# A Fourier token mixer with a hardswish MLP on one core: when the inverse transform's last stage runs, and where its two copies stand on ScalarE

## The chip, the cores and the metric

One core of one Trainium2 chip runs the whole kernel in float32. The metric is the device time in microseconds (us) of one execution. Engines are named as the profile names them: PE is TensorE (PEld its weight loads), ACT is ScalarE, DVE is VectorE, POOL is GpSimd, SP is SyncE, whose queue issues most of the DMAs.

## The reference, cut to what matters

```
x: 8 x 3008 x 256, filt_r and filt_i: 1505 x 256
y = irfft(rfft(x, axis=1) * (filt_r + 1j * filt_i), n=3008, axis=1)
t = y.reshape(24064, 256)
h = t @ w_in                               # 256 x 2048
g = h * clip(h + 3, 0, 6) / 6
out = g @ w_out                            # 2048 x 256
```

## The kernel before, in words

**The MLP sets the pace.** The 24064 tokens go in 47 blocks of 512 (256 pairs of tokens), numbered 0 to 46, and the 2048 hidden columns in 8 slices of 256. One block with one slice is a *step*; the steps 0 to 7 of a block follow each other, 376 in all. Both products of a step are done as 2x2 block products with seven multiplications (Strassen's scheme); block 0 alone is done plainly. The main loop (L1100 to L1160) writes each engine's order out by hand: within a step, the first product's parts for this step (`up_1` to `up_5`) alternate with the second product's parts for the step before (`down`). In PE's order: `up_1` (three products, into the PSUM tiles al and be), the early items of the plan (see below), `down` 1, `up_2` (two products), `down` 2 and 4, `up_3` (one product), `down` 5 and 6, `up_5` (one product, the "A22 product"), `down` 7 and 3.

The other engines' part of a step:

- ACT: L699 and L700 copy al and a half of be after `up_1`, L709 copies al after `up_2`; `relu(0)` (L733) follows in `up_4`; L728 copies al after the A22 product and `relu(1)` (L733) follows.
- DVE: first what the step before still owes, `g_sums`: hswish of the second half (L738) and the sums of g (L745, L746, L748). Then L714 (be plus s gives h, which `relu(0)` reads), L719 (al plus s5), and hswish of the first half (L738). The A22 product overwrites al, so it waits until L719 has read it.

**The mixer runs inside the MLP's steps.** The transform of length 3008 = 47 x 64 is done in stages for one of the eight sequences while the MLP works on the one before. A plan (`at(step, ...)`, L896) hangs its units on steps: an *early* item is issued after `up_1`, the others at the step's end. The units are:

- first stage: `a_unit` (PE, ACT), `a_sums` (DVE), `z_store` (four DMA issues on POOL's queue);
- second stage: `b_unit` (PE into two PSUM banks of the pool psF), `f_unit` (the filter: L515, L516, L517 on DVE, which read the banks and one operand in SBUF), `y_unit` (L526, L527 on DVE, both operands in SBUF), `bi_unit` (PE into two psF banks, two ACT copies) and `g_store` (DMA issues on POOL);
- last stage: `t4_load` (SP), then `n_five` for a chunk of five columns (5 x 47 pairs) or `n_unit` for a smaller one.

`n_five` takes both banks of psF, does 80 small products (L628), copies the two banks into the ring xn with ACT (`ring`, L610: two copies, or four where the ring wraps), and where the chunk completes a block it calls `ready`, which runs `t_sums` on POOL: seven additions (L684, tile xt) that the block's MLP steps need. The first of them reads the halves that both copies write. All of it is early, so the two copies stand in ACT's order between L700 and L709.

psF has two banks in all; `b_unit`, `bi_unit`, `a_unit`, `n_unit` and `n_five` take turns on them.

**Where the chunks stand.** Each block has a letter (`kinds`): the six blocks ahead of a new sequence are c, a, A, B, A, B, others count as a. A and B are the blocks in which the second stage stands: in A, `b_unit` at steps 2 and 6, `f_unit` at 2, 3, 6, 7, `y_unit` at 4 and 5; in B, `b_unit` at 4, `f_unit` at 4 and 5, `y_unit` at 2, 3, 6, 7, and `bi_unit` at 0 and 6 (and at step 1 of the A block that follows). `FIVE_AT` (L1029) gives the step of a five-column chunk by the letter: a chunk alone in its block, the first of two, the second of two. There are 46 such chunks: 12 in A blocks at step 4, 9 in B blocks at step 2, one in a B block (block 37) at step 3, the others in blocks of other letters or first of two.

In block 1 POOL also forms the sums of the weights (`w_sums`: L361 on POOL, L364 on ACT, which waits for L361); they stand at the ends of steps.

Of the kernel before, what the change touches and what calls it, by code (L numbers as in the profile page):

```python
# [34 lines left out]
B = 8  # L35
# [16 lines left out]
PAIRS = BLK // 2  # L52
# [129 lines left out]
def kernel(  # L182
# [64 lines left out]
    st = {}  # L247
# [330 lines left out]
    def pair(i):  # L578
        b, js, o, n = chunks[i]
        return b * HC * NA + o, n  # L580
# [24 lines left out]
    def ring(i, a, m_, to, out, src):  # L605
        done = 0
        while done < m_:
            r = (chunks[i][0] * HC * NA + to + done) % RING
            m = min(m_ - done, RING - r)
            nc.scalar.activation(out=out(ds(r, m)), in_=src[:, :, ds(a + done, m)], func=AXT.Copy)  # L610
            done += m

    def ready(i):
        t, n = pair(i)
        if (t + n) // PAIRS > t // PAIRS > 0:
            t_sums(t // PAIRS)


    def n_five(i):
        b, js, o, n = chunks[i]  # L620
        s0 = i % 2 * NJ
        ps = [psF.tile([P, 512], FP32, name="psn", tag="f")[:, 0:2 * n].rearrange("p (e n) -> p e n", e=2) for c in range(2)]
        for q, j in enumerate(js):
            for dh in range(2):
                for g in range(2):
                    for c in range(2):
                        r = ds(c * HALF, ATOM)
                        nc.tensor.matmul(ps[c][ts(g, HALF), dh, ts(q, NA)], t4[r, s0 + q, ds(dh * P + g * HALF, HALF)],  # L628
                                         groups[r, j, :], start=True, stop=True)
        for c in range(2):  # L630
            ring(i, 0, n, o, lambda at_: xn[:, :, c, at_], ps[c])
        ready(i)

    def n_unit(i, dh):
        ps = psF.tile([P, 512], FP32, name="psn", tag="f")
# [41 lines left out]
    def t_sums(k):  # L677
        t = xtp.tile([P, 5, PAIRS], FP32, name="xt")
        c0, s0, c1, s1 = (xb(k, d, c) for d in range(2) for c in range(2))
        u, v = (t[:, i, :] for i in (F5, F3))  # L680
        f1, f2, f3, f4, f5 = (t[:, i, :] for i in (F1, F2, F3, F4, F5))
        for o, x0, x1, op_ in ((f1, c0, s0, ALU.subtract), (u, c0, c1, ALU.add), (v, s0, s1, ALU.add),
                               (f4, u, v, ALU.subtract), (f5, u, v, ALU.add), (f2, c1, s1, ALU.add), (f3, f1, f2, ALU.add)):
            nc.gpsimd.tensor_tensor(out=o, in0=x0, in1=x1, op=op_)  # L684
        st["xt", k] = t

    def product(ps, p, w, x, start=False, stop=False):
        nc.tensor.matmul(ps, w_in[p][:, w, :], x, start=start, stop=stop, skip_group_check=True)  # L688
# [14 lines left out]
    def up_2(k, p):  # L703
        t = st["xt", k]
        al, be, s, s5 = st["up"]
        h = [hp.tile([P, 512], FP32, name="h%d" % i) for i in range(2)]
        product(al, p, S2, t[:, F3, :])
        product(be[:, 1, :], p, S4, t[:, F5, :], stop=True)
        nc.scalar.activation(out=s[:, 1, :], in_=al, func=AXT.Copy)  # L709
        st["h"] = h  # L710
# [10 lines left out]
    def up_4(k, p):  # L721
        st["g", k, p] = gp.tile([P, 7, 256], FP32, name="g")
        relu(0)
# [7 lines left out]
    def relu(i):  # L731
        r = rp.tile([P, 512], FP32, name="r", tag="r")
        nc.scalar.activation(out=r, in_=st["h"][i], func=AXT.Relu, bias=half_c, scale=1.0 / 6.0)  # L733
        st["r", i] = r
# [33 lines left out]
    def last_down():  # L768
        p, v, add = NP - 1, nc.vector.tensor_tensor, ALU.add
        g, o = st["g", LAST, p], st["o", LAST][0]  # L770
        hswish(LAST, p, 1)
        ps = [psF.tile([P, 512], FP32, name="psf", tag="f") for t in range(2)]
        for i, a in ((0, G11), (1, G12)):
            for t in range(2):
                for u in range(2):
                    nc.tensor.matmul(ps[t][:, ts(u, D)], g[:, a + t, ts(u, P)],
                                     w_out[p][:, 2 * i:2 * i + 2, :].rearrange("p j m -> p (j m)"),
                                     start=i == 0 and u == 0, stop=i == 1, skip_group_check=True)
        out_4(LAST)
        v(out=o_at(LAST, 0, 1), in0=st["po", LAST][3][:, 1, :, :], in1=o_at(LAST, 0, 1), op=add)  # L780
        for t, qs in ((0, (nc.sync, nc.gpsimd, nc.scalar)), (1, (nc.sync, nc.scalar))):
            both = o[:, t, :, :].rearrange("p u d -> p (u d)")
            v(out=both, in0=ps[t], in1=both, op=add)
            store_last(t, qs)
# [6 lines left out]
    def plain_up(p):  # L791
        st["g", 0, p] = gp.tile([P, 7, 256], FP32, name="g")
        st["h"] = [psU.tile([P, 512], FP32, name=n) for n in ("al", "be")]
        for i in range(2):
            for d in range(2):
                nc.tensor.matmul(st["h"][i], w_in[p][:, 2 * d + i, :], xn[:, d, :, 0:PAIRS], start=d == 0, stop=d == 1)
            relu(i)
            hswish(0, p, i)

    def plain_down(p):  # L800
        g = st["g", 0, p]
        if p == 0:
            st["po", 0] = [psO.tile([P, 2, 2, P], FP32, name="po%d" % i) for i in range(2)]
        for t in range(2):
            for u in range(2):
                for i, a in ((0, G11), (1, G12)):
                    nc.tensor.matmul(st["po", 0][t][:, u, :, :].rearrange("p a m -> p (a m)"), g[:, a + t, ts(u, P)],
                                     w_out[p][:, 2 * i:2 * i + 2, :].rearrange("p j m -> p (j m)"),
                                     start=p == 0 and u == 0 and i == 0, stop=p == NP - 1, skip_group_check=True)
# [82 lines left out]


    EARLY = (a_unit, b_unit, bi_unit, n_unit, n_five)

    def at(step, fn, *a):  # L896
        plan.setdefault((step, fn in EARLY), []).append((fn, a))

    with tc.manual_schedule():
# [126 lines left out]
                kinds[first[n] - 7 + d] = kind  # L1026

        N_AT = {"c": ((6, 6), (3, 3), (6, 6)), "a": ((2, 4), (2, 4), (6, 6)), "A": ((4, 5), (1, 1), (4, 5)), "B": ((2, 3), (1, 1), (2, 3))}
        FIVE_AT = {"c": (6, 3, 6), "a": (4, 2, 4), "A": (4, 0, 4), "B": (2, 1, 3)}  # L1029
        N_FIRST = {0: ((3, 4),), 1: ((), (2, 2), (3, 3)), 2: ((1, 1),), 3: ((1, 1),)}  # L1030
        in_block = {}
        for i in range(2, len(chunks)):
# [2 lines left out]
        for i in range(2, len(chunks)):  # L1035
# [3 lines left out]
            at_, kind = same.index(i) + 1 if len(same) > 1 else 0, kinds.get(k - 1, "a")  # L1039
            steps = N_FIRST[k - 1][at_] if k - 1 in N_FIRST else (FIVE_AT[kind][at_],) * 2 if len(chunks[i][1]) == NJ else N_AT[kind][at_]  # L1040
            if head and len(same) == 1:
# [58 lines left out]
        for i in range(len(items) + 1):  # L1100
            up = i < len(items)
            k, p = items[min(i, len(items) - 1)]
            dn = i > 0
            kd, pd = items[i - 1]
            def do(early):
                for fn, a in plan.get((i, early), ()):
                    fn(*a)

            if k == 0:
                plain_up(p)  # L1110
                do(True)
                if dn:
                    plain_down(pd)
                do(False)
                continue
            if not up:
                last_down()
                break
            up_1(k, p)
            ends = k == LAST and p == NP - 1  # L1120
            do(True)
            last_plain = dn and kd == 0
            dn = dn and kd > 0
            if dn:
                g_sums(kd, pd)
                down(kd, pd, 1)
            if up:
                up_2(k, p)
            if dn and pd == 0 and kd > 1:
                out_4(kd - 1)  # L1130
            if up:
                up_2b(k, p)
            if dn:
                down(kd, pd, 2, 4)
                if pd == NP - 1:
                    out_1(kd)
            if up:
                up_3(k, p)
            if dn:
                down(kd, pd, 5, 6)  # L1140
            if up:
                up_4(k, p)
            if ends:
                out_1(k)
            if last_plain:
                plain_down(pd)
                plain_out()
            if dn and pd == 0 and kd > 1:
                out_5(kd - 1)
            if up:  # L1150
                hswish(k, p, 0)
            if up:
                up_5(k, p)
            if dn:
                if pd == NP - 1 or ends:
                    out_2(kd)
                down(kd, pd, 7, 3)
                if pd == NP - 1 or ends:
                    out_3(kd)
            do(False)  # L1160
# [30 lines left out]
```

## Time and profile before

| what | value |
|---|---|
| three runs | 2677.99, 2678.18, 2678.54 us (median 2678.18) |
| the profiled execution | 2678.58 us, of which span 2676.8 us (first to last instruction) |
| granted PE clock | 1.000 |
| L733 ACT, relu, x736 | 721 ns each |
| L738 DVE, hswish, x736 | 716 ns each on average |
| L745, L746, L748 DVE, sums of g, x367 each | 470, 696, 435 ns on average |
| L526, L527 DVE, `y_unit`, x84 each | 810, 812 ns on average |
| L684 POOL, `t_sums`, x184 and x138 | 805, 1008 ns on average |
| L610 ACT, 128 x 470, x62 | 561 ns each |

How to read it: the profile's groups give the mean of one instruction; the timeline gives each instruction's start and duration in us from the start of the span ("x2" merges two in a row; in brackets stands the idle time before it and what ended it). The chain that ended last is followed back from the last instruction: at each step to what released it. A step begins with the first product of `up_1`, a PE row "al<-xt ... x2" that comes just ahead of a row "be<-xn"; the distance from one such row to the next is the step's length. A matmul's end is modelled.

### The profile page before, as it was taken

To read this page: it belongs to the slowest core of one execution; us is meant where nothing else is said; L and a number is where in the kernel's file an instruction comes from. 1 tells how busy PE (TensorE), PEld (TensorE's weight loads), DVE (VectorE), ACT (ScalarE), POOL (GpSimd) and SP (SyncE) were. 2 spreads that over 40 slices of the span, in tenths; PEclk is the share of its full clock that TensorE was granted. 3 is DMA by queue.
4 is the path that set the end of the run, shared out by engine and by line. 5 is a ranking of instruction groups with operands and counts; after the bars stand their busy time and mean duration, and the time that the engine had idled before them with its cause. 6 is when DMAs were issued, how large, how long until landed. Compare 5 with 4: busy or idle time off the path is not lost.

```text
span 2676.8 us, 54235 instructions
## 1 busy us (share of the span) xinstructions
PE 2646.1 (99%) x21584; PEld 2317.4 (87%) x21584; DVE 2062.9 (77%) x3503; ACT 1303.9 (49%) x2672; POOL 509.7 (19%) x731
## 2 busy tenths in 40 slices
PE   8999999999999999999999999999999999999999
PEld 6588888888888888888888888888888888899998
DVE  7878877887678876788767887678887788866666
ACT  3344454444544454444554444545454454454554
POOL 2251122111221112211122111311112111111110
PEclk9999999999999999999999999999999999999999
DMA  9732233212332123321233112331123321110000
GB/s 242 215 96 71 54 105 104 64 36 61 93 105 63 36 63 91 106 63 39 64 91 108 56 40 71 83 108 56 40 72 82 108 59 39 52 42 18 23 21 24
DMA packets 134819, 198.25 MB, mean 74 GB/s; under 512 B 23146, under 2 KB 99016, under 8 KB 134374
## 3 DMA queue, kind: packets, MB, share of 16 engines
q1 hardware_dynamic: 117037, 150.12, 19.8%
q0 software_dynamic: 16960, 44.16, 6.3%
q8 instruction: 170, 2.79, 0.4%
q14 instruction: 83, 0.68, 0.1%
q10 hardware_dynamic: 569, 0.50, 0.1%
HBM read 122.43 MB, written 83.98 MB: 77 GB/s over the span
## 4 chain that ended last, share of the span: by engine, by line
PE 88%; DVE 8%; DMA 1%; issue 1%; ACT 0%; POOL 0%; SPq 0%; DVEq 0%; POOLq 0%; ACTq 0%
PE po L764 40%; PE al L688 22%; PE be L688 16%; PE psn L628 2%; PE psf L538 2%; PE psf L447 2%; DVE g L738 2%; PE psf L494 1%; DVE y L526 1%; DVE y L527 1%; DVE g L745 1%; DVE h L714 1%; DVE h L719 1%; DVE g L746 1%; DMA w_all<-in_x_dram 1%
## 5 line engine op out<-in xcount | busy, mean ns | idle before, releaser
L764 PEld LDWEIGHTS po<-w_all,g 128*128 128x128 f32 x10276 | 1361.2, 191 | 154.7 <-issue 44.1
L764 PE MATMUL po<-w_all,g 128*128 128x128 f32 x10276 | 1402.5, 277 | 0.4 <-DVE g L738 0.2
L733 ACT ACTIVATE r<-h,half_c 128x512 f32<-128x512 f32 x736 | 531.0, 721 | 365.0 <-DVE h L714 352.9
L738 DVE SCALAR_TENSOR_TENSOR g<-r,h 128x512 f32<-128x512 f32 x736 | 526.7, 716 | 209.8 <-ACT r L733 195.6
L688 PE MATMUL al<-xt,w_all 128*128 128x256 f32 x2208 | 660.0, 381 | 3.7 <-ACT s L699 2.4
L688 PE MATMUL be<-xt,w_all 128*128 128x256 f32 x1472 | 437.9, 379 | 0.0
L714 DVE TENSOR_TENSOR h<-be,s 128x512 f32<-128x512 f32 x368 | 253.8, 690 | 166.5 <-PE be L688 161.7
L688 PEld LDWEIGHTS al<-xt,w_all 128*128 128x128 f32 x2208 | 335.2, 192 | 5.5 <-ACT s L699 3.0
L688 PEld LDWEIGHTS be<-xt,w_all 128*128 128x128 f32 x1472 | 279.7, 190 | 37.9
L728 ACT ACTIVATE h<-al 128x256 f32<-128x256 f32 x368 | 141.0, 383 | 325.8 <-PE al L688 325.8
L719 DVE TENSOR_TENSOR h<-al,s 128x256 f32<-128x256 f32 x368 | 155.8, 423 | 153.5 <-PE al L688 152.4
L746 DVE TENSOR_TENSOR g<-g 128x512 f32<-128x512 f32 x367 | 255.3, 696 | 12.6
L684 POOL TENSOR_TENSOR xt<-xn 128x256 f32<-128x256 f32 x184 | 144.6, 805 | 548.4 <-ACT xn L610 548.4
L709 ACT ACTIVATE s<-al 128x256 f32<-128x256 f32 x368 | 141.1, 383 | 194.6 <-PE al L688 190.9
L688 PE MATMUL al<-xn,w_all 128*128 128x256 f32 x736 | 222.6, 384 | 10.5 <-DVE h L719 10.5
L700 ACT ACTIVATE s<-be 128x256 f32<-128x256 f32 x368 | 141.0, 383 | 175.0 <-PE be L688 175.0
L688 PE MATMUL be<-xn,w_all 128*128 128x256 f32 x736 | 219.0, 379 | 0.0
L745 DVE TENSOR_TENSOR g<-g 128x256 f32<-128x256 f32 x367 | 172.3, 470 | 12.6
L554 POOL DMA_DIRECT2D g_tmp<-t x96 | 55.6, 593 | 648.1 <-ACT t L541 648.1
L699 ACT ACTIVATE s<-al 128x256 f32<-128x256 f32 x368 | 140.9, 383 | 67.3 <-PE al L688 67.3
L748 DVE TENSOR_TENSOR g<-g 128x256 f32<-128x256 f32 x367 | 159.6, 435 | 12.5
L468 POOL DMA_DIRECT2D z_tmp<-t x192 | 95.1, 504 | 364.6 <-DVE t L461 347.4
(149 smaller groups left out, 1869.3 us busy)
## 6 DMA issues: line engine op xcount, KB each, us to landing
g_tmp<-t POOLq DMA_DIRECT2D x96, 256.0 KB, 3.7
t<-g_tmp SPq DMA_DIRECT2D x184, 120.0 KB
t<-z_tmp SPq DMA_DIRECT2D x42, 512.0 KB
z_tmp<-t POOLq DMA_DIRECT2D x192, 96.0 KB, 2.5
xs<-in_x_dram SPq DMA_DIRECT2D x112, 128.0 KB
o_tmp<-o SPq DMA_DIRECT2D x46, 256.0 KB
ft<-in_filt_r_dram SPq DMA_DIRECT2D x168, 64.0 KB
ft<-in_filt_i_dram SPq DMA_DIRECT2D x168, 64.0 KB
```

Of the source, the lines that this page charges most:

```text
L684: nc.gpsimd.tensor_tensor(out=o, in0=x0, in1=x1, op=op_)
L688: nc.tensor.matmul(ps, w_in[p][:, w, :], x, start=start, stop=stop, skip_group_check=True)
L700: nc.scalar.activation(out=s5, in_=be[:, 1, :], func=AXT.Copy)
L709: nc.scalar.activation(out=s[:, 1, :], in_=al, func=AXT.Copy)
L714: nc.vector.tensor_tensor(out=st["h"][0].rearrange("p (a n) -> p a n", a=2), in0=be, in1=s, op=ALU.add)
L719: nc.vector.tensor_tensor(out=st["h"][1][:, 256:512], in0=al, in1=s5, op=ALU.add)
L733: nc.scalar.activation(out=r, in_=st["h"][i], func=AXT.Relu, bias=half_c, scale=1.0 / 6.0)
L738: nc.vector.scalar_tensor_tensor(out=st["g", k, p][:, o:o + 2, :].rearrange("p a n -> p (a n)"), in0=st["r", i], scalar=1.0, in1=st["h"][i ...
L745: v.tensor_tensor(out=g[:, G1, :], in0=g[:, G3, :], in1=g[:, G22, :], op=ALU.add)
L746: v.tensor_tensor(out=g[:, G3:G2 + 1:2, :], in0=g[:, G3:G1 + 1, :], in1=g[:, G11:G11 + 1, :].broadcast_to([P, 2, 256]), op=ALU.subtract)
L748: v.tensor_tensor(out=g[:, G4, :], in0=g[:, G12, :], in1=g[:, G2, :], op=ALU.subtract)
L764: nc.tensor.matmul(st["po", k][bank][:, part, u, :], g[:, a, ts(u, P)], w_out[p][:, w, :], start=(p == 0 and n in OPENS and u == 0), stop= ...
```

## The change

`FIVE_AT` moves a lone (or second) chunk of five columns one step on: from 4 to 5 in A blocks, from 2 to 3 in B blocks. `t4_load` of the chunk after next moves with it, being placed by the step of the chunk whose buffer it takes. And `n_five` no longer issues its copies itself; it leaves them in `st["leave"]`, and the main loop issues the first behind `up_2` (that is behind L709 on ACT) and the second, with `ready`, behind `up_4` (behind `relu(0)`). Chunks that fill block 0 or 1 keep the copies where they were. So 45 of the 46 chunks have their copies moved, and 21 of these change their step.

```diff
+        def leave(c):
             ring(i, 0, n, o, lambda at_: xn[:, :, c, at_], ps[c])
-        ready(i)
+            if c:
+                ready(i)
+        st["leave"] = [leave, leave]
+        if pair(i)[0] // PAIRS < 2:
+            for c in range(2):
+                leave(c)
+            st.pop("leave")
+
+    def leave(c):
+        if st.get("leave"):
+            st["leave"].pop()(c)
...
-        FIVE_AT = {"c": (6, 3, 6), "a": (4, 2, 4), "A": (4, 0, 4), "B": (2, 1, 3)}
+        FIVE_AT = {"c": (6, 3, 6), "a": (4, 2, 4), "A": (5, 0, 5), "B": (3, 1, 3)}
...
             if up:
                 up_2(k, p)
+            leave(0)
             if dn and pd == 0 and kd > 1:
                 out_4(kd - 1)
...
             if up:
                 up_4(k, p)
+            leave(1)
             if ends:
                 out_1(k)
```

(The removed line `for c in range(2):` ahead of `ring` is part of the first hunk.)

More of the change, by code (lines that the diff above doesn't have):

```diff
@@ L629, in n_five @@
                                          groups[r, j, :], start=True, stop=True)
-        for c in range(2):
+        def leave(c):
             ring(i, 0, n, o, lambda at_: xn[:, :, c, at_], ps[c])
-        ready(i)
+            if c:
[8 more added lines that the diff above has]
+            st["leave"].pop()(c)
     def n_unit(i, dh):
```

## The prediction, made before the changed kernel was run

> **What bounds the kernel now.** First the page's busy shares and the chain that ended last.
>
> ```profile
> PE 2646.1 (99%) x21584; PEld 2317.4 (87%) x21584; DVE 2062.9 (77%) x3503; ACT 1303.9 (49%) x2672; POOL 509.7 (19%) x731
> ...
> PE 88%; DVE 8%; DMA 1%; issue 1%; ACT 0%; POOL 0%; SPq 0%; DVEq 0%; POOLq 0%; ACTq 0%
> ```
>
> TensorE is the bound, and the only other engine on the chain with a share worth having is VectorE. To see where, I read the timeline of TensorE and took each step's length as the time from its first `al<-xt` row to that of the next step. Lengths repeat to a few ns: a bare step 6.15 us, one with `n_five` 7.66, one with `b_unit` (and `f_unit`) 7.365, one with `bi_unit` 7.365 to 7.46. A bare step with `f_unit` alone is 6.15, one with `y_unit` alone too, if nothing is left over from the step before. The exceptions are the steps just after `n_five` and `y_unit` together (step 5 of an A block, step 3 of a B block): 6.88 in place of 6.15. The A step before it is 7.755, 0.10 over 7.656. Here is the chain of waits of one such pair, block 31 (step 2 starts at 1827.08, step 3 at 1834.74, step 4 at 1841.62):
>
> ```profile
> 1832.72 0.42 DVE h L719
> 1833.15 0.60 DVE g L738
> ...
> 1833.78 1.11 DVE y L526
> ...
> 1834.91 1.12 DVE y L527
> ...
> 1836.13 1.04 DVE g L738
> ...
> 1837.19 0.85 DVE g L745
> ...
> 1838.06 0.70 DVE g L746
> ...
> 1839.81 0.34 DVE h L719
> ...
> 1840.20 0.70 PE al L688 x2
> ```
>
> VectorE runs without a pause, and the A22 product waits for its L719. The same operations last 0.69 (L526, L527, L738) and 0.42 (L745) elsewhere. The POOL timeline of the same stretch says why they are slow:
>
> ```profile
> 1831.04 2.10 POOL L684 TENSOR_TENSOR xt<-xn 128x256 f32<-128x256 f32 x3 [6.00 <-ACT xn L610]
> 1833.22 2.25 POOL L684 TENSOR_TENSOR xt<-xt 128x256 f32<-128x256 f32 x2
> 1835.44 1.17 POOL L684 TENSOR_TENSOR xt<-xn 128x256 f32<-128x256 f32 x1
> 1836.69 1.06 POOL L684 TENSOR_TENSOR xt<-xt 128x256 f32<-128x256 f32 x1
> ```
>
> These seven additions are `t_sums`. They start when the copies of `n_five` (L610) end. The first three meet only L714 and L719, which keep their 0.69 and 0.42; the last four alternate with L526, L527, L738 and L745, and both sides stretch.
>
> **The skill on this.** The Trainium skill, "SBUF — State Buffer", section "Who interferes with whom", says that a VectorE instruction with two SBUF inputs contends with a GpSimd instruction that reads SBUF, that the lock is held for a whole instruction and the other blocks, and that one with at most one SBUF input (outside the two-port modes) doesn't. The trace agrees on both halves: L714 and L719 read PSUM and stay at 0.69 and 0.42 beside L684; L526 (two SBUF inputs) goes from 0.69 to 1.10. The rule names L746 and L748 too, which are undisturbed above. Block 17 shows them: there `t_sums` starts late (at 1069.39), being queued behind four `z_store` issues on POOL.
>
> ```profile
> 1072.73 0.83 DVE L745 TENSOR_TENSOR g<-g 128x256 f32<-128x256 f32 x1
> 1073.59 1.10 DVE L746 TENSOR_TENSOR g<-g 128x512 f32<-128x512 f32 x1
> 1074.72 0.83 DVE L748 TENSOR_TENSOR g<-g 128x256 f32<-128x256 f32 x1
> ```
>
> So a later `t_sums` meets more of the sums of g. From L745's end to L746's end it takes 1.13 (1073.56 to 1074.69), to L748's end 0.86 more. I go by these rows.
>
> **The change, part by part.**
> *The copies.* Nothing is added: the same L610 copies (about 0.56 each, or two parts together some 0.75 where the ring wraps). The first now stands between L709 (ends 4.28 us after the step's start) and `relu(0)` (L733, starts 5.11 after it): ACT sits idle there for 0.84. The second stands between `relu(0)` and L728, where ACT idles 1.13. Both fit, so I cost them at nothing on ACT; if one overran, `relu(0)` or L728 would be late by the excess. L709 gains nothing: it waits for S2 at that point either way. But the second copy can't start before `relu(0)` is over, and `t_sums` needs both copies: f1 reads both column halves. In block 31 `relu(0)` ends at 1832.91, the copy near 1833.5; `t_sums` starts there, not at 1831.04.
> *The psF banks* come free 2.5 us later, still long before the next step's `b_unit`, `bi_unit` or `a_unit` (1.2 us after its start): nothing. *SP*: `t4_load` moves one step with its chunk and is wanted some 14 steps later; the queue's other loads keep their order: nothing.
>
> *The shift by one step*, 12 A blocks (4 to 5) and 9 B blocks (2 to 3). The step it leaves holds `y_unit` alone. In B that is a bare 6.148 (block 37, whose chunk stands there already, shows 6.148). In A `f_unit` is left over: L517 ends 1.44 after the start; then L738, L745, L746, L748 (0.72, 0.46, 0.72, 0.46 with gaps), L714, and L719 ends at 4.86. The A22 weight load stands at 4.72 in a bare step and follows L719 by 0.06: 0.20 late, step 6.35. The 0.10 of psF waiting goes: `n_five` no longer follows `f_unit` directly. The step it enters: 7.656.
>
> *The step after it* now holds `b_unit`: 7.365, 1.217 more cover than the bare one had. On block 31's times: POOL's first addition gets the lock after L738, at 1833.74, the place that the fourth had. From there the alternation is that of the trace, up to L745's end at 1838.03, with four additions done. Three are left. By block 17's figures L746 ends at 1839.16, L748 at 1840.02, L714 at 1840.74, L719 (0.60 after L714's start, 0.41 long) at 1841.06, weight load 1841.12. Due: 1834.74 + 4.72 + 1.217 = 1840.68. **0.44 late**: 7.805.
> *What is late next*: `f_unit` starts at once after the late `hswish(0)`, and the next step, bare with another `f_unit`, has no cover. Its L517 ends 1.67 after its start, L719 at 5.09, due 4.66: 0.43 late, 6.578. In the step after that `bi_unit` waits for psF until L517 has ended, 1.67 after its start. The trace has 7.456 where L517 ended at 1.44 and 7.637 at 1.62 (block 37), so 7.69.
> A: 6.348 + 7.656 + 7.805 + 6.578 + 7.69 = 36.08; before 7.756 + 6.882 + 7.365 + 6.148 + 7.456 = 35.61: +0.47, times 12 = **+5.6**.
> B: 6.148 + 7.656 + 7.805 + 6.578 + 7.69 = 35.88; before 7.656 + 6.882 + 7.365 + 6.148 + 7.459 = 35.51: +0.37, times 9 = 3.3, less 0.2 for block 7's step 3 (7.117 before): **+3.1**. Block 37, in place already, loses 0.44 + 0.43 + 0.05 = **+0.9**.
>
> *Chunks that only have their copies delayed.* In c and a blocks an `a_unit` step follows (7.37, its L719 due at 5.88 or later; mine ends near 5.5): nothing. Four at the end (blocks 40 to 43) have a bare step behind. In block 40 L738 ends at 2355.79; three additions to 2357.77, then L738, L745, L746 and L748, one addition ahead of each: 2358.31, 2359.17, 2360.30, 2361.16; L719 at 2362.20, load 2362.26, due 2361.51: 0.75 each, **+3.0**. In block 1 the weight sums (L361) queue on POOL behind `t_sums`; ACT's L364 waits for them, L699 for L364, and TensorE for L699: 1.96 idle now, at 168.14. With seven additions from 162.62, four of them alternating, `t_sums` ends at 168.57 and L361 starts there, not at 165.39: **+3.2**. Blocks 2 and 3 (steps of 8.01 and 8.02 at 201.77 and 261.15): L748 (0.86, 0.83) no longer meets POOL, which frees 0.35 each; the collisions go to the next step, where I make it 0.35 and 0.85: **+0.5**, bounds -0.7 and +2.
>
> Sum 5.6 + 3.1 + 0.9 + 3.0 + 3.2 + 0.5 = +16.3. On the profiled execution (span 2676.8, its time 2678.58): 2694.9. The median shown, 2678.18, is 0.4 lower: 2694.5.
>
> Two costs are not seen as they will stand: seven additions in alternation with L746 and L748 after a `y_unit`, and a late VectorE across two `f_unit` steps. From below: if nothing beyond L745 collides, A loses its 0.63 and B 0.73. From above: if every addition delayed VectorE by a whole 0.59 once more, each of the 22 places costs about 0.4 more, +9.
>
> **Rivals.**
> *Faster: the cover is enough.* `b_unit`'s 1.217 us takes in the backlog of 0.735. Block 37 speaks for it: chunk at step 3, then 7.365 and 6.148, and only `bi_unit` 0.18 late. There `t_sums` starts at 2170.57, 3.6 after the step's start. If the delayed copies leave it early enough that one addition fewer collides (0.57 is more than my 0.44), A gains 0.63 and B 0.73: -7.6 - 6.8, block 1 and the tail give back 3 to 6: 2668. It decides at a start about 0.6 us sooner than mine; `relu(0)` stands in front, and block 17 shows the collisions.
> *Collisions as forecast, but the small places don't follow* (block 1's weight sums, the tail): +8 to +10, 2687.
> *The backlog runs on* through `bi_unit` and the second `f_unit` pair: the upper bound, 2704.
> *The change doesn't do what it says*: ACT's order isn't the code's. In the trace it is, row for row; then only the shift would count, near 2667 to 2678.
>
> **The numbers.** Forecast 0.66, small places missing 0.14, backlog 0.08, cover enough 0.08, no effect 0.04. Range 2685 to 2702: it leaves out the faster case, no effect and most of the backlog case. A measurement tells about 0.2% (5.4 us) from no change: faster 0.08, same 0.05, slower 0.87.
>
> **What would show it.** Right: L684 starts 6.3 to 6.5 us into the step, behind `relu(0)`; L746 at 1.10 and L748 at 0.83 in the `b_unit` step after; that step near 7.8 and the next near 6.58; the `y_unit` step 6.35 in A; TensorE waiting for L699 some 5 us in block 1. Wrong: `b_unit` steps at 7.365, L746 at 0.69, or `t_sums` starting before `relu(0)` ends.

## The result, and the profile after

| | before | after |
|---|---|---|
| runs, median | 2678.36 us (2677.99 to 2679.01, 4 runs) | 2693.18 us (2691.56 to 2693.84, 4 runs) |
| ratio | | 1.0053, 95% interval 1.0041 to 1.0066 |
| span of the profiled execution | 2676.8 us | 2691.5 us |

The change costs 14.8 us; 2694.5 was forecast. The page of the kernel after, busy shares and chain:

```profile
PE 2659.1 (99%) x21584; PEld 2322.2 (86%) x21584; DVE 2088.6 (78%) x3503; ACT 1299.8 (48%) x2672; POOL 526.0 (20%) x731
...
PE 81%; DVE 13%; issue 2%; DMA 2%; ACT 1%; SPq 0%; POOL 0%; DVEq 0%; POOLq 0%; ACTq 0%
```

No instruction was added, yet DVE and POOL are busy for 26 and 16 us more, and DVE's share of the chain goes from 8% to 13%. (The new kernel's lines are 10 higher from `t_sums` on. L694 is `t_sums`, L698 the up products. On DVE, L724, L729, L748, L755, L756, L758 are what L714, L719, L738, L745, L746, L748 were; on ACT, L709, L719, L738, L743 are what L699, L709, L728, L733 were.) In block 31 the step with `n_five` now starts at 1843.09 and the `b_unit` step at 1850.75. POOL's timeline there:

```profile
1849.43 3.19 POOL L694 TENSOR_TENSOR xt<-xn 128x256 f32<-128x256 f32 x3 [14.52 <-ACT xn L610]
1852.70 1.92 POOL L694 TENSOR_TENSOR xt<-xt 128x256 f32<-128x256 f32 x2
1854.58 1.17 POOL L694 TENSOR_TENSOR xt<-xn 128x256 f32<-128x256 f32 x1
1855.83 0.79 POOL L694 TENSOR_TENSOR xt<-xt 128x256 f32<-128x256 f32 x1
```

`t_sums` starts 6.34 us into the step, where it started 3.96 in, and its first three additions, which took 2.10, take 3.19. DVE's timeline beside it:

```profile
1849.79 1.10 DVE L526 TENSOR_TENSOR y<-s 64x512 f32<-64x512 f32 x1
1850.92 1.11 DVE L527 TENSOR_TENSOR y<-s 64x512 f32<-64x512 f32 x1
1852.13 1.03 DVE L748 SCALAR_TENSOR_TENSOR g<-r,h 128x512 f32<-128x512 f32 x1
1853.20 0.83 DVE L755 TENSOR_TENSOR g<-g 128x256 f32<-128x256 f32 x1
1854.07 1.10 DVE L756 TENSOR_TENSOR g<-g 128x512 f32<-128x512 f32 x1
1855.20 0.83 DVE L758 TENSOR_TENSOR g<-g 128x256 f32<-128x256 f32 x1
1855.96 0.68 DVE L724 TENSOR_TENSOR h<-be,s 128x512 f32<-128x512 f32 x1
1856.56 0.41 DVE L729 TENSOR_TENSOR h<-al,s 128x256 f32<-128x256 f32 x1
```

The first four are as slow as before. The next two are slow too; in the kernel before they were not, and the PSUM reader L714 followed:

```profile
1838.06 0.69 DVE L746 TENSOR_TENSOR g<-g 128x512 f32<-128x512 f32 x1
1838.78 0.43 DVE L748 TENSOR_TENSOR g<-g 128x256 f32<-128x256 f32 x1
1839.13 0.68 DVE L714 TENSOR_TENSOR h<-be,s 128x512 f32<-128x512 f32 x1
```

The two that read PSUM (L724, L729) are not slowed. Each of the six slow ones is 0.34 to 0.42 longer than alone, whatever its width. The step lengths (first `al<-xt` row to first `al<-xt` row) add up to the loss. Differences to the kernel before, us:

| where | forecast | after |
|---|---|---|
| 12 A blocks, five steps each | +5.6 | +4.33 |
| 9 B blocks, five steps each | +3.1 | +2.43 |
| block 37 | +0.9 | +0.81 |
| the four places at the end | +3.0 | +2.58 |
| block 1 | +3.2 | +4.05 |
| blocks 2 and 3 | +0.5 | +0.07 |
| all other steps | 0 | -0.01 |
| sum | +16.3 | +14.26 |

What stands ahead of the MLP is the same code in both kernels, but its length differs from execution to execution: over all profiled executions shown here the first step of block 1 starts anywhere from 128.5 to 131.4 us. Sums over steps leave that out. The differences of medians don't: here and in the experiments they lie 0.2 to 1.4 us off the sums.

### The profile page after: what moved, and what is told of

The parts are those of the page before. It is cut to its first block, busy times and chain, and to the rows that moved or that the text cites. A ratio compares the mean times of both kernels' runs of the same rounds, so it can differ in the third digit from the quotient of the medians.

```text
span 2691.5 us, 54276 instructions
## 1 busy us (share of the span) xinstructions
PE 2659.1 (99%) x21584; PEld 2322.2 (86%) x21584; DVE 2088.6 (78%) x3503; ACT 1299.8 (48%) x2672; POOL 526.0 (20%) x731
## 4 chain that ended last, share of the span: by engine, by line
PE 81%; DVE 13%; issue 2%; DMA 2%; ACT 1%; SPq 0%; POOL 0%; DVEq 0%; POOLq 0%; ACTq 0%
PE po L774 37%; PE al L698 21%; PE be L698 15%; DVE g L748 2%; PE psn L628 2%; PE psf L538 2%; PE psf L447 2%; DVE g L756 2%; DVE h L724 1%; DVE g L755 1%; DVE y L526 1%; DVE y L527 1%; ACT r L743 1%; DVE h L729 1%; DVE s L517 1%
## 5 line engine op out<-in xcount | busy, mean ns | idle before, releaser
L743 ACT ACTIVATE r<-h,half_c 128x512 f32<-128x512 f32 x736 | 530.9, 721 | 368.5 <-DVE h L724 356.5
L748 DVE SCALAR_TENSOR_TENSOR g<-r,h 128x512 f32<-128x512 f32 x736 | 523.3, 711 | 220.5 <-ACT r L743 206.4
L698 PE MATMUL al<-xt,w_all 128*128 128x256 f32 x2208 | 660.5, 381 | 6.3 <-ACT s L709 4.9
L698 PE MATMUL be<-xt,w_all 128*128 128x256 f32 x1472 | 438.3, 379 | 0.0
L724 DVE TENSOR_TENSOR h<-be,s 128x512 f32<-128x512 f32 x368 | 253.5, 689 | 154.3 <-PE be L698 148.7
L698 PEld LDWEIGHTS al<-xt,w_all 128*128 128x128 f32 x2208 | 335.5, 192 | 8.0 <-ACT s L709 5.6
L694 POOL TENSOR_TENSOR xt<-xn 128x256 f32<-128x256 f32 x184 | 181.2, 1002 | 761.7 <-ACT xn L610 761.7
L698 PEld LDWEIGHTS be<-xt,w_all 128*128 128x128 f32 x1472 | 280.0, 190 | 38.0
L756 DVE TENSOR_TENSOR g<-g 128x512 f32<-128x512 f32 x367 | 271.0, 738 | 12.6
L719 ACT ACTIVATE s<-al 128x256 f32<-128x256 f32 x368 | 141.1, 383 | 288.6 <-PE al L698 288.3
L738 ACT ACTIVATE h<-al 128x256 f32<-128x256 f32 x368 | 141.0, 383 | 287.8 <-PE al L698 287.7
L729 DVE TENSOR_TENSOR h<-al,s 128x256 f32<-128x256 f32 x368 | 155.2, 422 | 143.5 <-PE al L698 142.8
L698 PE MATMUL al<-xn,w_all 128*128 128x256 f32 x736 | 226.4, 389 | 8.6 <-DVE h L729 7.2
L698 PE MATMUL be<-xn,w_all 128*128 128x256 f32 x736 | 219.0, 379 | 0.0
L758 DVE TENSOR_TENSOR g<-g 128x256 f32<-128x256 f32 x367 | 174.7, 476 | 12.5
L755 DVE TENSOR_TENSOR g<-g 128x256 f32<-128x256 f32 x367 | 173.1, 472 | 12.6
L709 ACT ACTIVATE s<-al 128x256 f32<-128x256 f32 x368 | 140.9, 383 | 67.4 <-PE al L698 67.4
L698 PEld LDWEIGHTS be<-xn,w_all 128*128 128x128 f32 x736 | 139.8, 190 | 19.0 <-DVE g L748 0.2
```

Source lines behind the costliest of these rows:

```text
L724: nc.vector.tensor_tensor(out=st["h"][0].rearrange("p (a n) -> p a n", a=2), in0=be, in1=s, op=ALU.add)
L729: nc.vector.tensor_tensor(out=st["h"][1][:, 256:512], in0=al, in1=s5, op=ALU.add)
L748: nc.vector.scalar_tensor_tensor(out=st["g", k, p][:, o:o + 2, :].rearrange("p a n -> p (a n)"), in0=st["r", i], scalar=1.0, in1=st["h"][i ...
L755: v.tensor_tensor(out=g[:, G1, :], in0=g[:, G3, :], in1=g[:, G22, :], op=ALU.add)
L756: v.tensor_tensor(out=g[:, G3:G2 + 1:2, :], in0=g[:, G3:G1 + 1, :], in1=g[:, G11:G11 + 1, :].broadcast_to([P, 2, 256]), op=ALU.subtract)
L758: v.tensor_tensor(out=g[:, G4, :], in0=g[:, G12, :], in1=g[:, G2, :], op=ALU.subtract)
```

## The experiments

The theory to test: the loss is the lock between POOL's reads and DVE's second SBUF input, met by a `t_sums` that the second copy makes late; the shift by itself is a gain. The rivals: the shift is what costs; or lateness as such, whoever waits.

**The shift alone** (e1_shift_only), the kernel before with one line changed:

```diff
-        FIVE_AT = {... "A": (4, 0, 4), "B": (2, 1, 3)}
+        FIVE_AT = {... "A": (5, 0, 5), "B": (3, 1, 3)}
```

> The shift by one step alone: FIVE_AT as in the changed kernel, the two copies where they were before, so that t_sums starts about 3.6 us into the step. Theory (the late second copy, through t_sums and the lock on VectorE's second SBUF input, eats more than the shift gains): the b_unit step after the chunk has cover enough, 7.365, and only bi_unit is 0.18 late, as in block 37 of the kernel before; an A block gains 0.46, a B block 0.56 (0.8 in block 7): -5.5 - 5.2 = -10.7, 2667.6 us. Rival (the shift itself is what costs, since it puts n_five beside y_unit and ahead of b_unit): slower than before, near 2693 less the 7 that block 1 and the end of the kernel cost, 2686 us.

Measured: 2668.01 us (5 runs), ratio 0.9962 (0.9950 to 0.9975). By steps A -5.35, B -4.98, all else 0. The `b_unit` step is at 7.365 and the next at 6.15 (6.22 in three places); `bi_unit` is 0.18 late nearly everywhere. The shift is a gain of 10 us; the rival falls.

**The copies alone** (e2_copies_only), the changed kernel with the old `FIVE_AT`:

> The copies alone: placed as in the changed kernel, FIVE_AT as before. Theory: every step behind n_five and y_unit is bare and its L719 comes 1.55 late, 7.70 in place of 6.88: +0.82 in each of the 21 places, +17.2; block 37 +0.8, the tail +2.6, blocks 1 to 3 +4.1: +24.5, 2702.9 us, slower than the changed kernel. Rival (late copies cost nothing by themselves, only beside b_unit): block 1 and the tail alone, +7, 2685 us.

Measured: 2703.43 us (4 runs), ratio 1.0095 (1.0082 to 1.0109). The step behind `n_five` and `y_unit` takes 7.70 (6.88 before) in all 21 places: A +9.83, B +7.10, the rest as in the changed kernel. So the two parts pull in opposite directions, -10 and +25, and nearly add: what is left is the +15 of the result.

**The same work on POOL without the reads** (e3_write_only), the changed kernel with

```diff
-            nc.gpsimd.tensor_tensor(out=o, in0=x0, in1=x1, op=op_)
+            if o is f1:
+                nc.gpsimd.tensor_tensor(out=o, in0=x0, in1=x1, op=op_)
+            else:
+                nc.gpsimd.memset(t[:, 2:5, :] if o is f3 else t[:, 0:3, :], 0.0)
```

> The changed kernel, with six of the seven additions of t_sums replaced by memsets of about the same length (three columns' slices of the tile, some 0.67 us each); the first addition stays and so waits for the second copy. The block sums are not computed, so the output is not the reference's; order, waits and the length of POOL's work stay. Theory (POOL's reads of SBUF block VectorE's second input): L746 and L748 at 0.69 and 0.42 everywhere, y_unit at 0.69, the b_unit steps 7.365, the f_unit steps 6.15, the tail steps 6.15: -7.7 in A, -6.8 in B, -0.2 in block 37, about -1.2 in blocks 2 and 3, block 1 still 1.5 to 3.5 late: 2664.5 us. Rival (lateness as such: whatever waits for the late copies or the late t_sums): 2693 us as the changed kernel.

Measured: 2664.00 us (4 runs), ratio 0.9949 (0.9934 to 0.9964). POOL's timeline in block 31, and DVE's:

```profile
1827.62 0.91 POOL L695 TENSOR_TENSOR xt<-xn 128x256 f32<-128x256 f32 x1 [14.52 <-ACT xn L610]
1828.59 4.71 POOL L697 MEMSET xt<- 128x768 f32 x6
```

```profile
1827.98 1.10 DVE L526 TENSOR_TENSOR y<-s 64x512 f32<-64x512 f32 x1
1829.12 0.69 DVE L527 TENSOR_TENSOR y<-s 64x512 f32<-64x512 f32 x1
...
1831.09 0.69 DVE L759 TENSOR_TENSOR g<-g 128x512 f32<-128x512 f32 x1
1831.82 0.43 DVE L761 TENSOR_TENSOR g<-g 128x256 f32<-128x256 f32 x1
```

POOL starts as late as in the changed kernel and works for 5.7 us, but only L526, which meets the one addition left, is slow. By steps A is at -7.58 and B at -6.82 (forecast -7.7 and -6.8), the tail at 0, block 37 at -0.18, blocks 2 and 3 at -1.60. Behind these chunks lateness by itself costs nothing; the reads do. Block 1 is the exception: it stays at +3.49. There lateness does cost, because the weight sums queue on POOL behind `t_sums` whatever `t_sums` does, and TensorE is idle for 3.75 us.

**Block 1** (e4_block1_early), the changed kernel with

```diff
-        if pair(i)[0] // PAIRS < 2:
+        if pair(i)[0] // PAIRS < 3:
```

> The changed kernel, but the two chunks that fill block 2 (issued in steps 2 and 3 of block 1) keep their copies where they were before. Theory (block 1's loss of 4.2 us is the late t_sums ahead of the weight sums in POOL's order, plus TensorE at half clock after 4.3 us without work): the b_unit step behind is back at 9.04 with 1.8 us of idle, no slow matmuls follow, and 4.2 us are given back: 2689.0 us. Rival (the loss is ACT's, which must do the copies between relu and the weight scaling): the step stays near 13.3, 2693 us.

Measured: 2688.90 us (4 runs), ratio to before 1.0040 (1.0026 to 1.0054). Block 1 is at -0.01, all else as in the changed kernel. So block 1's loss comes from the late copies of these chunks. By itself this doesn't part the two explanations, since the edit takes the copies off ACT at that place as well as starting `t_sums` sooner. The changed kernel's trace does: ahead of the weight scaling (L364) ACT has nothing to do and waits for POOL's L361, so the rival falls.

```profile
169.40 0.31 ACT L364 ACTIVATE w_all<-w_all 128x128 f32<-128x128 f32 x1 [4.95 <-POOL w_all L361]
```

**A way round the lock** (e5_split_sums): the shift, the copies where they were, and `t_sums` in two parts for the shifted chunks and block 37's.

```diff
+    def t_rest(k, p):
+        g = st["g", k, p][:, G4, 0:4]
+        nc.gpsimd.tensor_tensor(out=gate, in0=g, in1=g, op=ALU.add)
+        for o, x0, x1, op_ in st.pop("rest4"):
+            nc.gpsimd.tensor_tensor(out=o, in0=x0, in1=x1, op=op_)
...
-        for o, x0, x1, op_ in (...):
+        now = 3 if split else 7
+        for o, x0, x1, op_ in sums[:now]:
             nc.gpsimd.tensor_tensor(out=o, in0=x0, in1=x1, op=op_)
+        if split:
+            st["rest4"] = sums[now:]
...
                 g_sums(kd, pd)
+                if late_sums:
+                    t_rest(kd, pd)
```

(`sums` is the tuple of the seven additions; `late_sums` is true in the step after `n_five`.)

> The shift, the copies where they were, and t_sums split for the shifted chunks (and block 37's): its first three additions at once, in the time in which VectorE works out of PSUM, the other four in the next step behind L748 (held there by a small addition that reads g's last sum), where VectorE again works out of PSUM. Theory of the lock: no addition meets a two-input instruction of VectorE for more than a moment, so y_unit and the sums of g keep 0.69 and 0.42, and the b_unit and bi_unit steps lose nothing: A gains 0.64, B 0.73, block 37 0.18: -14.7, 2663.7 us. Rival (POOL's additions cost VectorE time wherever they lie, or block starts wait for the later sums): no better than the shift alone, 2667 to 2675 us.

Measured: 2672.59 us (17 runs), ratio 0.9980 (0.9973 to 0.9987): a miss, and worse than the shift alone. POOL and DVE in the `b_unit` step of block 31:

```profile
1839.80 0.72 POOL L682 TENSOR_TENSOR xt<-xn 128x256 f32<-128x256 f32 x1
1840.60 0.73 POOL L682 TENSOR_TENSOR xt<-xt 128x256 f32<-128x256 f32 x1
```

```profile
1840.88 1.00 DVE L749 SCALAR_TENSOR_TENSOR g<-r,h 128x512 f32<-128x512 f32 x1
1841.80 0.68 DVE L516 TENSOR_TENSOR s<-psf,ft 128x512 f32<-128x512 f32 x1
```

I had expected no addition to meet a two-input instruction "for more than a moment". The last one starts 0.28 ahead of hswish(0) (L749) and holds the lock: 1.00 in place of 0.68. This 0.32 comes out as 0.08 in the second `f_unit` step and 0.30 in `bi_unit` (7.76 in place of 7.46), 21 times over.

**One addition moved** (e6_two_gates): as before, but the seventh addition waits for that hswish:

```diff
                 hswish(k, p, 0)
+                if late_sums:
+                    t_rest(k, p, G11, 1)
```

(One addition; the first gate releases three.)

> As e5_split_sums, but the seventh addition waits for hswish of the first half (L738) in the b_unit step, so that it falls into the time of f_unit, whose instructions read PSUM. Theory (in e5 that one addition held the lock when hswish(0) was due, 0.32 us, and the two f_unit steps without slack handed this on to bi_unit): f_unit steps back at 6.15 and bi_unit at 7.46: -14.7, 2663.5 us. Rival (the loss in e5 came with the additions' mere presence in that step): 2672 us as e5.

Measured: 2665.00 us (5 runs), ratio 0.9951 (0.9938 to 0.9965); A -6.53, B -6.23 by steps. The two timelines again, POOL and then DVE:

```profile
1835.79 0.20 POOL L680 TENSOR_TENSOR gate<-g 128x4 f32<-128x4 f32 x1 [1.04 <-DVE g L750]
1835.94 0.73 POOL L683 TENSOR_TENSOR xt<-xt 128x256 f32<-128x256 f32 x1
```

```profile
1835.03 0.68 DVE L750 SCALAR_TENSOR_TENSOR g<-r,h 128x512 f32<-128x512 f32 x1
1835.63 0.68 DVE L516 TENSOR_TENSOR s<-psf,ft 128x512 f32<-128x512 f32 x1
```

hswish is back at 0.68 and the addition runs beside `f_unit`, whose first operand is in PSUM, at full speed on both sides. Some 0.07 per `bi_unit` is left, and 0.42 behind block 20: together the 1.8 by which A and B fall short of their forecast. The 0.07 comes from hswish(0) of the second `f_unit` step, which starts 0.07 later after its step's start than in the kernel before, with `relu(0)` at the same place; a further wait, for POOL's read of g, is a likely reason, but was not tried. Why block 20 loses more is open.

**Block 1's order** (e7_sums_last): as e6, and `ready` for block 2 goes into the plan's late items, behind that step's `w_sums`.

> As e6_two_gates, and in block 1 t_sums for block 2 is issued behind that step's weight sums instead of ahead of them. Theory: ACT's L364 finds its sums done, L699 is in time, and the b_unit step of block 1 goes from 9.04 to about 7.1: 1.9 us less than e6, 2661.6 us. Rival (POOL is simply busy there and something else is late by as much): 2663.5 us.

Measured: 2662.65 us (5 runs), ratio 0.9944 (0.9931 to 0.9956). The `b_unit` step of block 1 takes 7.01 in place of 9.04, and block 1 is 2.18 shorter. The medians of e6 and e7 differ by 2.4, of which the steps account for 2.1. This version beats both kernels, the one before by 15.4 us.

## Why the prediction was right, point by point

*The copies cost ACT nothing*: right. In block 31 they lie between L719 (ends 1847.36) and `relu(0)`, and between `relu(0)` and L738. ACT has idle time left at both places:

```profile
1848.20 0.72 ACT L743 ACTIVATE r<-h,half_c 128x512 f32<-128x512 f32 x1 [0.33 <-DVE h L724]
...
1850.06 0.38 ACT L738 ACTIVATE h<-al 128x256 f32<-128x256 f32 x1 [0.63 <-PE al L698]
```

Both start as far into the step as before (5.11 and 6.97; the kernel before has them at 1832.19 and 1834.05).

*t_sums starts 6.3 to 6.5 in, and meets L746 and L748*: right, 6.34, and 1.10 and 0.83. That POOL's reads are the cause is shown by e3.

*The step it leaves*: 6.34 in A, 6.148 in B (6.35 and 6.148 forecast). *The step it enters*: 7.656, exact.

*The `b_unit` step after it*: 7.70, where 7.805 was forecast. The mechanism is right and its size was 0.11 too large: L724, which reads PSUM, starts at 1855.96, while L758 ends at 1856.03; I had put it 0.03 after that end. The kernel before has such an early start in block 31 too, beside an L748 that met nothing: it ends at 1839.21, and L714 starts at 1839.13 (rows above). *The two steps behind*: 6.575 and 7.688 (6.578 and 7.69 forecast). The 0.11 in each of 21 places is 2.3 us, more than the whole 2.0 by which the sum was off; the same 0.11 makes each place of the tail 0.65 in place of 0.75. (Block 7's `b_unit` step, where the kernel before had a longer step too, took 7.95.)

*Block 1*: the chain L694, L361, L364, L709, TensorE was right, its size 4.05 in place of 3.2, from two errors against each other; that it came so near is luck. TensorE's idle time grew by 2.56 (1.77 to 4.33), not 3.2: the weight sums, now behind everything, met no DVE instruction and were faster. But then the matmuls were slow. The row of the kernel before, then of the kernel after:

```profile
168.15 0.70 PE L688 MATMUL al<-xt,w_all 128*128 128x256 f32 x2 [1.77 <-ACT s L699]
```

```profile
171.10 1.20 PE L698 MATMUL al<-xt,w_all 128*128 128x256 f32 x2 [4.33 <-ACT s L709]
```

From this product to the third of the step, 1.85 pass in the kernel before (168.15 to 170.00) and 3.52 after (171.10 to 174.62): 1.7 more, which no term of the forecast had. The cause is TensorE's clock (last section).

*Blocks 2 and 3*: +0.07 for +0.5. The 0.35 each came back as forecast (7.656 for 8.01 and 8.02). The forecast took back 0.35 and 0.85 for the collisions behind them: block 3's step gives 0.77. Block 2's gives nothing: the sums of g are slow there too (L756 1.10 and L758 0.83, from 215.97), but the step keeps its 7.01, so it had room for them.

*The time itself* was met within 1.3 us, in part by luck: the steps lose 14.26 where 16.3 was forecast, and the medians differ by 0.6 more than the steps.

*The rival on the other side* (the cover is enough) was right in kind: with `t_sums` at its old start the `b_unit` step loses nothing. That its 2668 is also e1's median is chance. It was made of 0.63 and 0.73 gained per block, less 3 to 6 us for block 1 and the tail; e1 gains 0.45 and 0.55, as `bi_unit` is late, and loses nothing elsewhere.

## What to carry to other kernels

Ask of a moved copy who starts when it ends: these two copies cost ACT nothing, but the second holds back a GpSimd job by 2.4 us, into the time of VectorE's instructions with two SBUF inputs. A GpSimd job that reads SBUF belongs beside VectorE instructions that read PSUM; where it can't be kept short enough, split it and let each part wait for the last SBUF instruction ahead of such a stretch (e6). And when a combined change measures as a small loss, run its parts: here -10 and +25 were hidden in +15.

## What the runs showed of the hardware that was not expected

An idle time of 4.3 us halved TensorE's clock for what followed. The table of windows of the kernel after (window, its length, busy time and count of PE, PEld, DVE, ACT and POOL, granted PE clock, DMA share, GB/s):

```profile
166.00:171.00 5.00, 0.77 (x6) 0.56 (x4) 2.31 (x3) 0.84 (x4) 4.69 (x9) 1.00 0.15 35
171.00:172.00 1.00, 0.90 (x2) 0.81 (x3) 0.00 (x0) 0.32 (x2) 0.84 (x3) 0.58 0.00 0
172.00:173.00 1.00, 1.00 (x4) 0.73 (x4) 0.00 (x0) 0.38 (x1) 1.00 (x3) 0.50 0.00 0
173.00:174.00 1.00, 1.00 (x6) 1.00 (x5) 0.69 (x1) 0.02 (x1) 0.84 (x3) 0.50 0.00 0
174.00:175.00 1.00, 1.00 (x7) 0.97 (x6) 0.00 (x0) 0.70 (x1) 1.00 (x3) 0.72 0.00 0
```

The clock is at 0.50 from about 171.2 to 174.6, some 3.4 us, and the matmuls take 1.8 times as long (1.84 for the eight from 172.94, 1.05 elsewhere). After 1.75 us of idle in e4 the same product lasts 0.70 and the next ones are at full speed. In e3, after 3.75 us, that product is still at full speed, and the clock falls to 0.50 only 0.7 us later, at 168.78:

```profile
168.07 0.70 PE L701 MATMUL al<-xt,w_all 128*128 128x256 f32 x2 [3.75 <-ACT s L712]
...
169.29 1.91 PE L777 MATMUL po<-w_all,g 128*128 128x128 f32 x8
```

The Trainium skill, "TensorE: Matmul & The Clock Gate", section "What's actually happening", gives half rate after an idle window of about 3.4 us and again a busy window of that length before full rate. It also calls the window free-running. The clock's records in the traces agree on the length and on the free run: the slow stretch in block 1 lasts 3.413 us in all three runs that have one (the changed kernel, e2, e3), and in all nine traces every change of the clock comes a whole number of 3.413 us, within 0.01, after the first. They don't bear out that the whole window must be idle: the one that ended at 168.78 in e3 began at 165.37 and held 2.7 us of idle. So what a stall costs depends on how it lies against the window. Some executions of the changed kernel could escape the slow stretch; whether its fastest run (2691.56, 1.6 under the median) is one of them is not shown.
